# A Nystrom attention and two-layer FFN kernel: the first layer in blocks of 512 tokens across batches, and one store of PSUM banks

## The chip, the cores and the metric

The kernel runs on one core of a Trainium2 chip. The metric is the device time of one execution in microseconds, the median over the runs. Each engine (TensorE = PE, VectorE = DVE, ScalarE = ACT, GpSimd = POOL, and SyncE = SP, which issues all the DMAs here) works through its own list of instructions in a fixed order and waits for the others by semaphores.

## The reference, cut to what matters

Attention with 32 landmarks on 4 batches, 8 heads, 576 positions of 64 values, then two feed-forward layers on 2304 tokens (model width 512, hidden width 2048). All inputs are float64 in the reference.

```python
q_lm = q.reshape(B, H, m, S // m, D).mean(axis=3); k_lm = ...
A, Bm, C = sm(q, k_lm), sm(q_lm, k_lm), sm(q_lm, k)      # softmax of scaled scores
Z = Bm.transpose(0, 1, 3, 2) / (norm_1(Bm) * norm_inf(Bm) + 1e-06)
for _ in range(6):
    Z = 2 * Z - Z @ Bm @ Z
x = (A @ Z @ C @ v)                                      # [B, H, S, D] -> [2304, 512]
h = x @ moe_w_in;  x = (h * np.tanh(softplus(h))) @ moe_w_out
h = x @ moe2_w_in; return (h / (1 + np.exp(-h))) @ moe2_w_out
```

## The kernel before

**Attention** works on eight groups of four heads (`Group`, g = 0 to 7; two groups make a batch). A group loads k and q (`load`) and v (`load_v`), transposes k and q on TensorE (`transposed`, results `Tk` and `Tq`), sums nine pairs of rows into landmarks (`sums` on VectorE or POOL, or for groups 2 and 3 products with the constant `twice` on TensorE), takes scores, exponentials and maxima, and runs six Newton steps on a 32x32 system for each head (`newton`, tile `yu`). `c_side` multiplies the transposed exponentials `ect` with v (mark `cv`). The last product of a group has the operands `bd,yu`; it gives `ut`, the landmark values. `a_side` gives the query weights in a tile `at` for each batch.

**The first layer** never forms the attention output. `projection` multiplies `ut` of a batch with the weights `wa` into landmark weights `wp` (512 hidden columns at a time, a tile of 16 KB in each partition, ring of three). A unit (phase, token block t, hidden tile f) is then `emit_h` (`h<-at,wp`: six matmuls, two head groups times three passes, since every value is split into a high and a low part in the format fp32r, `PASSES`), `gated` (ACT activation `z`, its high part `g` on ACT, its low part on POOL) and `emit_o` (`y<-g,wo`: four output tiles times three passes, twelve matmuls). The hidden width is cut in two halves: phase 0 runs all token blocks over hidden tiles 0 to 7 and stores partial sums `yh`, phase 1 over 8 to 15, reads `yh` back and stores `ys`. A token block of phases 0 and 1 is half a batch, 288 tokens, so eight blocks; phase 2, the second layer, has blocks of 512 (`h<-x,wi`, `y<-wo,g`; four of 512 and one of 256). Weights come as float64 words and are put together by ACT and DVE (`decode`, tiles `m` and `wa`) and split by ACT and POOL.

**What sets the order.** A planner written into the kernel (`Line`) runs while the program is built: it holds a time for each engine and a cost for each instruction and emits what is ready next, so the order on each engine is fixed before the launch. Attention steps are chains that are stepped when their inputs are due; units of the first layer fill in when `h_time` and `o_time` say that they are ready. Where TensorE has nothing and its recent activity is low (`cold`), two transposes of the identity are put in (`y<-ident` and the like). Tiles come from `Ring`s: a taker waits until a slot is given back. PSUM has eight banks: four for `y`, two for `h`, two for attention (`t`); groups 0 and 1 borrow from `y` and `h`. Group 1's q and its transposes are put in the three `wp` slots (`borrow`).

Of the kernel before, what the change touches and what calls it, by code (L numbers as in the profile page):

```python
# [23 lines left out]
SLACK = 0.3  # L24
# [304 lines left out]

@with_exitstack  # L330
def kernel(
# [29 lines left out]
    NB = {0: 2 * B, 1: 2 * B, 2: -(-NT // 512)}  # L361
# [3 lines left out]
    def tokens(ph, t):  # L365
        return (t * SH, SH) if ph < 2 else (t * 512, min(512, NT - t * 512))
# [24 lines left out]
    wp_p = l1.enter_context(tc.tile_pool(name="wp", bufs=3))  # L391
    at_p = l1.enter_context(tc.tile_pool(name="at", bufs=1))
    z_p = l1.enter_context(tc.tile_pool(name="z", bufs=3))
    g_p = l1.enter_context(tc.tile_pool(name="g", bufs=4))
    ps_y = ctx.enter_context(tc.tile_pool(name="ps_y", bufs=4, space=bass.MemoryType.PSUM))
    ps_h = ctx.enter_context(tc.tile_pool(name="ps_h", bufs=2, space=bass.MemoryType.PSUM))
    pctx = ctx.enter_context(ExitStack())
    ps_t = pctx.enter_context(tc.tile_pool(name="ps_t", bufs=2, space=bass.MemoryType.PSUM))
# [142 lines left out]
    lent = []  # L541
    for b in (3, 2):
        words = at_p.tile([128, 4 * GB * SH], I32, tag=f"at{b}", name=f"aw{b}")
        lent += [words[:, i:i + 1024].rearrange("p (n t) -> p n t", t=2) for i in (0, 1024)]
# [14 lines left out]
    def projection(b, fb):  # L559
        keys = [("a", 0, fb * KD + kk) for kk in range(KD)]  # L560
        yield from until(lambda: wp_r.any() and all(w_ready.get(k, LATE) <= line.now for k in keys))
# [13 lines left out]
        wp_ = wp_t[b, fb] = wp_r.take([128, 2, GB, FB], F32R)  # L575
        wp = wp_[0]
        yield "W"
        for e in range(GB):
            VA.copy(out=wp[:, 0, e], in_=pp[e][0])
        yield "V"  # L580
        for e in range(GB):
            V.tensor_tensor(out=wp[:, 1, e], in0=pp[e][0], in1=f32(wp[:, 0, e]), op=ALU.subtract)
            Ring.give(pp[e])
        wp_ready[b, fb] = line.end + 0.12 + SLACK
        yield "W"

    def inputs():

        for t in range(NB[2]):
            n0, n = tokens(2, t)  # L590
            need = [("y", 1, i) for i in range(n0 // SH, -(-(n0 + n) // SH))]
# [17 lines left out]
    def emit_h(ph, t, f):  # L609
        h = h_t[ph, t, f] = h_r.take([128, 512], FP32)  # L610
        n = tokens(ph, t)[1]
        if ph < 2:
            b, e = divmod(t, 2)
            wp, at = wp_t[b, f // 4][0], a_t[b]
            ops = [
                (wp[:, i, k, f % 4 * 128:f % 4 * 128 + 128], at[:, j, k, e]) for k in range(GB) for i, j in PASSES
            ]
        else:
            wi = w_t["i", 1, f]
            ops = [  # L620
                (wi[:, i, k * 128:(k + 1) * 128], x_t[t][k][0][:, j, :n]) for k in range(KD) for i, j in PASSES
            ]
        for i, (w, x) in enumerate(ops):
            T.matmul(out=h[0][:, :n], lhsT=w, rhs=x, start=(i == 0), stop=(i == len(ops) - 1))
            if i % STRIDE == STRIDE - 1:
                yield

    def gated(ph, t, f):

        h = h_t.pop((ph, t, f))  # L630
        n = tokens(ph, t)[1]
        yield from until(z_r.any)
        z_ = z_r.take([128, SH if ph < 2 else 512], FP32)
# [5 lines left out]
        g = g_t[ph, t, f] = g_r.take([128, 2, SH if ph < 2 else 512], F32R)  # L639
# [6 lines left out]
    def emit_o(ph, t, f, first, last):  # L646
        n = tokens(ph, t)[1]
# [3 lines left out]
        if first:  # L651
            y_t[ph, t] = []
        for d in range(parts):
            if first:
                y_t[ph, t].append(y_r.take([128, 512], FP32))
# [16 lines left out]
    def partial(t):  # L672

        yp_t[t] = []
        n0, n = tokens(1, t)
        yield from until(marked(("part", 0, NB[0] - 1)))
# [6 lines left out]
    def finish(ph, t, d):  # L683
        n0, n = tokens(ph, t)
# [54 lines left out]
    class Group:  # L739
        def __init__(self, g):  # L740
            self.g = g
            self.b, self.hg = divmod(g, GB)

            self.banks = h_r if g == 1 else t_r
            self.pairs = y_r if g < 2 else t_r
            self.tT, self.lm = {}, {}

        def load(self):
# [4 lines left out]
            if self.g == 1:  # L753
                self.borrow()
                qn = self.borrowed[0][0][:, 0:J]
# [11 lines left out]
        def borrow(self):  # L767
            self.borrowed = [wp_r.take([128, 32, D], FP32) for i in range(3)]

        def load_v(self):  # L770
            vn = self.vn = qkv_p.tile([96, HG, VI, D], FP32, tag="vn", name="vn")
            src = heads(v, self.b, self.hg).rearrange("h (p i) d -> p h i d", i=VI)
            line.transfer(nc.sync, out=vn, in_=src)
            self.v_at = line.end

        def sums(self, nm, src):

            now, free = line.now, line.free
            lm = self.lm[nm] = s_p.tile([128, 2, D], FP32, tag="lm" + nm, name="lm" + nm)
            if max(now, free["V"]) + 3 < max(now, free["P"]) + 3.4:  # L780
                V.tensor_reduce(out=lm[:, 0, :], in_=src.rearrange("p j d -> p d j"), axis=AX.X, op=ALU.add)
                yield "V"
                V.copy(out=lm[:, 1, :], in_=lm[:, 0, :])
            else:
                t9 = s_p.tile([128, J2, D], FP32, tag="t9", name="t9", bufs=1)
# [471 lines left out]
```

## Time and profile before

| | us |
|---|---|
| median of 3 runs | 874.95 (874.9 to 878.39) |
| the profiled execution | 875.92 |
| its span, first to last instruction | 874.1 |
| TensorE busy | 847.2 (97%) |
| first layer, `y` matmuls, busy | 234.1 (1536 of them) |
| first layer, `h` matmuls, busy | 120.3 (768) |
| second layer, `y` / `h` matmuls, busy | 204.8 / 206.5 |

Attention takes up to about 222 us of the span, with the first layer woven in from 51 us on; the first layer then runs alone until 466 us, and the second layer from there. Matmul records overlap, since one begins before the one ahead of it has drained: a mean length is longer than the distance from start to start, which is what counts in a dense run. `PEld` rows are loads of the stationary operand; every matmul here has one.

### The profile page before, as it was taken

To read this page: it belongs to the slowest core of one execution; us is meant where nothing else is said; L and a number is where in the kernel's file an instruction comes from. 1 tells how busy PE (TensorE), PEld (TensorE's weight loads), DVE (VectorE), ACT (ScalarE), POOL (GpSimd) and SP (SyncE) were. 2 spreads that over 40 slices of the span, in tenths; PEclk is the share of its full clock that TensorE was granted. 3 is DMA by queue.
4 is the path that set the end of the run, shared out by engine and by line. 5 is a ranking of instruction groups with operands and counts; after the bars stand their busy time and mean duration, and the time that the engine had idled before them with its cause. 6 is when DMAs were issued, how large, how long until landed. Compare 5 with 4: busy or idle time off the path is not lost. (4 is left out here: it accounts for less than half of the span.)

```text
span 874.1 us, 15110 instructions
## 1 busy us (share of the span) xinstructions
PE 847.2 (97%) x6036; PEld 718.5 (82%) x6036; DVE 302.0 (35%) x574; ACT 383.8 (44%) x804; POOL 344.4 (39%) x335
## 2 busy tenths in 40 slices
PE   7999999899999999999999999999999999999997
PEld 6777766676999899999998876888888888888896
DVE  4966634543576872010118779300000000000000
ACT  5575767656565553342335445421232123212322
POOL 4241633432455672432337766531233123212221
PEclk8999999999999999999999999999999999999999
DMA  9774225200335532331136900120012000100000
GB/s 250 223 219 152 66 46 136 56 29 5 121 125 189 155 111 64 111 97 56 55 124 227 338 31 1 30 67 1 1 27 58 1 1 24 37 1 1 24 26 25
DMA packets 41863, 72.29 MB, mean 83 GB/s; under 512 B 5184, under 2 KB 29248, under 8 KB 41792
## 3 DMA queue, kind: packets, MB, share of 16 engines
q1 hardware_dynamic: 41792, 71.32, 27.0%
q8 instruction: 47, 0.77, 0.4%
q14 instruction: 24, 0.20, 0.1%
HBM read 57.15 MB, written 14.16 MB: 82 GB/s over the span
## 5 line engine op out<-in xcount | busy, mean ns | idle before, releaser
L221 POOL TENSOR_TENSOR g<-z,g 128x288 fp32r<-128x288 f32 (+2 forms) x208 | 208.1, 1008 | 385.3 <-ACT g L221 325.7
L221 PE MATMUL y<-g,wo 128*128 128x288 f32 x1536 | 234.1, 301 | 0.0
L221 ACT ACTIVATE z<-h 128x288 f32<-128x288 f32 (+2 forms) x208 | 96.0, 468 | 293.1 <-PE h L221 258.0
L221 PEld LDWEIGHTS y<-g,wo 128*128 128x128 f32 x1536 | 209.6, 188 | 12.9 <-issue 9.0
L221 PE MATMUL h<-x,wi 128*128 128x512 f32 (+1 forms) x960 | 206.5, 371 | 0.6 <-POOL wi L221 0.6
L221 PE MATMUL y<-wo,g 128*128 128x512 f32 x864 | 204.8, 392 | 1.2 <-POOL g L221 1.1
L221 PEld LDWEIGHTS h<-x,wi 128*128 128x128 f32 x960 | 167.7, 188 | 34.7 <-POOL wi L221 1.9
L221 PEld LDWEIGHTS y<-wo,g 128*128 128x128 f32 x864 | 161.5, 188 | 38.4 <-POOL g L221 2.5
L221 PE MATMUL h<-at,wp 128*128 128x288 f32 x768 | 120.3, 301 | 5.3 <-ACT z L221 5.2
L221 PEld LDWEIGHTS h<-at,wp 128*128 128x128 f32 x768 | 106.1, 188 | 19.2 <-issue 8.5
L221 ACT CAST g<-z 128x288 fp32r<-128x288 f32 (+2 forms) x204 | 98.2, 490 | 17.5 <-PE y L221 13.9
L221 DVE SCALAR_TENSOR_TENSOR m<-wst,m 128x512 int32<-128x512 int32 x96 | 105.3, 1115 | 1.6
L221 POOL TENSOR_TENSOR wo<-m,wo 128x512 fp32r<-128x512 f32 x32 | 48.2, 1508 | 35.5 <-ACT wo L221 32.0
L221 DVE CAST x<-xst 128x512 fp32r<-128x512 f32 (+1 forms) x4 | 2.9, 721 | 160.8 <-PE h L221 160.8
L221 DVE TENSOR_SCALAR m<-m 128x512 int32<-128x512 int32 x48 | 34.5, 724 | 31.0 <-ACT m L221 31.0
L221 ACT ACTIVATE m<-wst 128x512 f32<-128x512 f32 x48 | 32.4, 675 | 24.8 <-POOL wo L221 11.1
L221 DVE TENSOR_TENSOR ysb<-y,ysb 128x288 f32<-128x288 f32 x32 | 13.3, 457 | 80.5 <-PE y L221 77.1
L221 ACT ACT_TABLE_LOAD x31 | 39.8, 1283 | 1.7 <-PEq L1241 0.7
L221 POOL TENSOR_TENSOR x<-xst,x 128x512 fp32r<-128x512 f32 (+1 forms) x20 | 24.7, 1234 | 35.1 <-ACT x L221 35.1
L221 DVE TENSOR_TENSOR wp<-t,wp 128x512 fp32r<-128x512 f32 x32 | 20.6, 686 | 39.7 <-ACT wp L221 39.6
L221 POOL TENSOR_TENSOR wi<-m,wi 128x512 fp32r<-128x512 f32 x16 | 24.6, 1535 | 14.8 <-ACT wi L221 14.3
L221 ACT CAST wp<-t 128x512 fp32r<-128x512 f32 x31 | 16.7, 590 | 28.8 <-PE t L221 28.8
(159 smaller groups left out, 549.2 us busy)
## 6 DMA issues: line engine op xcount, KB each, us to landing
wst<-in_moe_w_out_dram SPq DMA_DIRECT2D x32, 512.0 KB, 6.5
wst<-in_moe_w_in_dram SPq DMA_DIRECT2D x28, 512.0 KB, 6.2
kn<-in_k_dram SPq DMA_DIRECT2D x32, 144.0 KB, 5.0
vn<-in_v_dram SPq DMA_DIRECT2D x8, 576.0 KB, 6.2
yh<-ysb SPq DMA_DIRECT2D x32, 144.0 KB, 1.9
ysb<-yh SPq DMA_DIRECT2D x32, 144.0 KB, 2.5
ys<-ysb SPq DMA_DIRECT2D x32, 144.0 KB, 2.2
out_dram<-ysb SPq DMA_DIRECT2D x72, 64.0 KB, 1.7
```

The costliest lines, as they stand in the source:

```text
L221: r = getattr(self.nc[e], name)(**kw)
```

## The change

1. Token blocks of phases 0 and 1 are 512 tokens as in phase 2 (`tokens`): four of 512 and one of 256 instead of eight of 288. A block may lie across a batch border; `pieces` cuts it there, and `emit_h` runs its six matmuls for each piece into its own columns of one PSUM bank. The cuts are 512 | 64, 448 | 128, 384 | 192, 320 | 256. A block that touches two batches needs the landmark weights and query weights of both.
2. Landmark weights are kept in halves of 256 hidden columns, in a ring of seven tiles of 8 KB (`WP`) instead of three of 16 KB.
3. All eight PSUM banks are one store (`Banks`); `h`, `y`, attention (`t`) and the idle transposes take from it up to a limit each (`Share`): `h` two (four in phase 2), `y` four, `t` three, or seven where nothing of the first layer is ready, idle one.
4. Group 1's q and its transposes lie in the tiles of the query weights of batches 0 and 1 (`aw`), its v in two tiles of the gating ring `g`. The `z` ring has two tiles for three and the `g` ring three for four, since they are wider.
5. From group 2 on v is loaded by a chain of its own (`later_v`) after the `cv` of the group before, into a single tile. `sums` runs on VectorE alone.

```diff
+class Share:
+    def ready(self, n=1):
+        return len(self.banks.free()) >= n and self.banks.held(self.kind) + n <= self.most()
...
-    def tokens(ph, t):
-        return (t * SH, SH) if ph < 2 else (t * 512, min(512, NT - t * 512))
+    def tokens(t):
+        return t * 512, min(512, NT - t * 512)
+    def pieces(t):
+        n0, n = tokens(t)
+        cuts = sorted({n0, n0 + n} | {b * S for b in range(B) if n0 < b * S < n0 + n})
+        return [(a // S, a % S, a - n0, c - a) for a, c in zip(cuts, cuts[1:])]
...
-    h_r, y_r, ysb_r = Ring("h", ps_h, 2), Ring("y", ps_y, 4), Ring("ysb", y_p, YSB)
-    z_r, g_r, wp_r = Ring("z", z_p, 3), Ring("g", g_p, 4), Ring("wp", wp_p, 3)
-    t_r = Ring("t", ps_t, 2)
+    h_r = Share("h", banks, lambda: 4 if grown else 2)
+    y_r = Share("y", banks, lambda: KD)
+    clock_r = Share("idle", banks, lambda: 1)
+    t_r = Share("t", banks, lambda: 3 if busy() else 7)
+    z_r, g_r, wp_r = Ring("z", z_p, 2), Ring("g", g_p, 3), Ring("wp", wp_p, WP)
...
-            b, e = divmod(t, 2)
-            wp, at = wp_t[b, f // 4][0], a_t[b]
-            ops = [
-                (wp[:, i, k, f % 4 * 128:f % 4 * 128 + 128], at[:, j, k, e]) for k in range(GB) for i, j in PASSES
-            ]
+            ops = []
+            for b, at, to, m in pieces(t):
+                wp, a = wp_t[b, f // 2][0], a_t[b].rearrange("p i k e n -> p i k (e n)")
+                ops += [
+                    (wp[:, i, k, f % 2 * 128:f % 2 * 128 + 128], a[:, j, k, at:at + m], slice(to, to + m), (k, i, j))
+                    for k in range(GB) for i, j in PASSES
+                ]
...
-            if max(now, free["V"]) + 3 < max(now, free["P"]) + 3.4:
-                V.tensor_reduce(out=lm[:, 0, :], in_=src.rearrange("p j d -> p d j"), axis=AX.X, op=ALU.add)
...
+            V.tensor_reduce(out=lm[:, 0, :], in_=src.rearrange("p j d -> p d j"), axis=AX.X, op=ALU.add)
...
-                groups[n].load_v()
+                line.add(groups[n].later_v(), "C")
...
-        return max([wp_ready.get((t // 2, f // 4), LATE)] + [a_ready.get((t // 2, e), LATE) for e in range(GB)])
+        of = [b for b, *_ in pieces(t)]
+        return max([wp_ready.get((b, f // 2), LATE) for b in of] + [a_ready.get((b, e), LATE) for b in of for e in range(GB)])
```

Three places show how the instructions move. In the rows `at_` with a number is the query weight tile of one batch, and `x` at the end counts instructions.

TensorE in phase 1, batches 0 and 1, before, where attention is long done:

```order
L221 MATMUL y<-g,wo 128x288 x36
L221 MATMUL h<-at_1331,wp 128x288 x30
L221 MATMUL y<-g,wo 128x288 x36
L221 MATMUL h<-at_1331,wp 128x288 x6
L221 MATMUL y<-g,wo 128x288 x24
```

The same place after the change (`at_724` is batch 0, `at_1376` batch 1; the block of 512 tokens ends batch 0 after 64):

```order
L221 MATMUL h<-at_724,wp 128x512 x18
L221 MATMUL h<-at_724,wp 128x64 x6
L221 MATMUL h<-at_1376,wp 128x448 x6
L221 MATMUL h<-at_724,wp 128x64 x6
L221 MATMUL h<-at_1376,wp 128x448 x6
L221 MATMUL y<-g,wo 128x512 x2
L221 MATMUL t<-wa,ut_154 32x512 x8
L221 MATMUL y<-g,wo 128x512 x58
```

Every `h` of a block on a border is now two runs of six matmuls, one narrow and one wide, and `y` is wide.

TensorE around the end of group 3 (`bd,yu`), which finishes batch 1, before:

```order
L221 MATMUL t<-yu 32x64 x4
L221 MATMUL h<-at_634,wp 128x288 x2
L221 MATMUL y<-g,wo 128x288 x2
L221 MATMUL t<-Tk,lmT 32x288 x8
L221 MATMUL y<-g,wo 128x288 x20
L221 MATMUL t<-bd,yu 64x128
L221 MATMUL y<-g,wo 128x288 x4
```

And after:

```order
L221 MATMUL h<-at_724,wp 128x512 x2
L221 MATMUL idle<-ident 128x128 x4
L221 MATMUL t<-yu 32x64 x4
L221 MATMUL idle<-ident 128x128 x6
L221 MATMUL t<-ident,lmk 128x128
L221 MATMUL t<-ident,lmq 128x128
L221 MATMUL idle<-ident 128x128 x8
L221 MATMUL y<-g,wo 128x512 x2
L221 MATMUL t<-bd,yu 64x128
L221 MATMUL y<-g,wo 128x512 x6
L221 MATMUL t<-wa,ut_154 32x512 x8
```

Idle transposes now stand where first-layer matmuls of batch 0 stood: the first block is through, and the next one needs batch 1.

VectorE at the start (`lmk`, `lmq` are the landmark sums of k and q, `nmb` the first maximum of a group), before:

```order
L221 TENSOR_REDUCE lmk<-kn 128x64
L221 COPY lmk<-lmk 128x64
L221 TENSOR_REDUCE lmk<-kn 128x64
L221 COPY lmk<-lmk 128x64
L221 TENSOR_REDUCE nmb<-t 128x1
```

And after:

```order
L221 TENSOR_REDUCE lmk<-kn 128x64
L221 TENSOR_REDUCE lmq<-qn 128x64
L221 TENSOR_REDUCE lmk<-kn 128x64
L221 TENSOR_REDUCE lmq<-aw_157 128x64
L221 COPY lmk<-lmk 128x64
L221 COPY lmq<-lmq 128x64
L221 COPY lmk<-lmk 128x64
L221 COPY lmq<-lmq 128x64
L221 TENSOR_SCALAR lmT<-t 128x128 x2
L221 TENSOR_REDUCE nmb<-t 128x1
```

The two sums of q came from POOL to VectorE, and the copies of both groups stand behind all four sums.

## Rows read from the trace of the kernel before

**Rows 1.** The page, parts 1 and 2: all engines, and TensorE's granted clock.
```profile
PE 847.2 (97%) x6036; PEld 718.5 (82%) x6036; DVE 302.0 (35%) x574; ACT 383.8 (44%) x804; POOL 344.4 (39%) x335
PEclk8999999999999999999999999999999999999999
```

**Rows 2.** Groups by shape, first layer on TensorE: busy us, mean ns, idle before.
```profile
L221 PE MATMUL y<-g,wo 128*128 128x288 f32 x1536 | 234.1, 301 | 0.0
...
L221 PE MATMUL h<-at,wp 128*128 128x288 f32 x768 | 120.3, 301 | 5.3 <-ACT z L221 5.2
```

**Rows 3.** Timeline of TensorE, first layer alone: start us, length us, instructions.
```profile
340.19 6.56 PE L221 MATMUL y<-g,wo 128*128 128x288 f32 x48
346.59 0.95 PE L221 MATMUL h<-at,wp 128*128 128x288 f32 x6
```

**Rows 4.** Timeline of TensorE in the second layer, and one piece of the chain.
```profile
599.85 8.54 PE L221 MATMUL y<-wo,g 128*128 128x512 f32 x36
608.22 8.32 PE L221 MATMUL h<-x,wi 128*128 128x512 f32 x36
616.38 8.32 PE L221 MATMUL y<-wo,g 128*128 128x512 f32 x36
...
834.15 5.91 PE L221 MATMUL h<-x,wi 128*128 128x256 f32 x48
839.90 5.76 PE L221 MATMUL y<-wo,g 128*128 128x512 f32 x24
...
561.37 2.72 PE y L221 x12
```

**Rows 5.** Timeline of TensorE, Newton steps of attention between first-layer matmuls.
```profile
215.08 1.06 PE L221 MATMUL y<-g,wo 128*128 128x288 f32 x6
216.07 0.37 PE L221 MATMUL t<-yu 32*32 32x96 f32 x8
216.37 1.06 PE L221 MATMUL y<-g,wo 128*128 128x288 f32 x6
```

**Rows 6.** Weight loads (PEld): three stretches of the timeline, and the group.
```profile
215.08 0.83 PEld L221 LDWEIGHTS y<-g,wo 128*128 128x128 f32 x6
...
210.69 1.10 PEld L221 LDWEIGHTS y<-g,wo 128*128 128x128 f32 x8
...
42.75 2.09 PEld L221 LDWEIGHTS t<-Tk,twice 128*128 128x128 f32 x18
...
L221 PEld LDWEIGHTS y<-g,wo 128*128 128x128 f32 x1536 | 209.6, 188 | 12.9 <-issue 9.0 <-POOL g L221 0.2
```

**Rows 7.** Timeline of TensorE, a run of idle transposes.
```profile
48.65 1.75 PE L221 MATMUL y<-ident 128*128 128x128 f32 x14
```

**Rows 8.** What TensorE waited for: us in total, times, longest.
```profile
PE t L221 <- ACT ec L221: 6.6, 6, 1.5
PE h L221 <- ACT z L221: 5.2, 7, 1.0
```

**Rows 9.** Timeline of VectorE at the start.
```profile
5.53 2.14 DVE L221 TENSOR_REDUCE lmk<-kn 128x64 f32<-128x1152 f32 x1 [3.89 <-DMA kn<-in_k_dram]
...
15.94 0.19 DVE L221 TENSOR_REDUCE nmb<-t 128x1 f32<-128x32 f32 x1 [3.08 <-PE t L221]
```

**Rows 10.** Groups by shape: gating of 512 columns on ACT and POOL.
```profile
L221 ACT CAST g<-z 128x512 fp32r<-128x512 f32 x63 | 39.2, 622 | 1.7
L221 ACT ACTIVATE z<-h 128x512 f32<-128x512 f32 x64 | 38.2, 598 | 182.6 <-PE h L221 153.4 <-POOL g L221 25.1 <-POOL wi L221 4.1
...
L221 POOL TENSOR_TENSOR g<-z,g 128x512 fp32r<-128x512 f32 x64 | 86.0, 1344 | 176.0 <-ACT g L221 135.6 <-issue 29.7 <-PE h L221 9.6
```

**Rows 11.** Timelines of SP's queue and of TensorE: group 2's v.
```profile
24.52 0.33 SPq L232 DMA_DIRECT2D vn<-in_v_dram  x1
...
63.88 0.88 PE L221 MATMUL t<-vn,ect 96*32 96x64 f32 x48
```

More of the change, by code (lines that the diff above doesn't have):

```diff
@@ L327, in give, with __init__, held, free @@
         tile[1][2].append(max(x[2] for k in "wr" for x in Ring.line.seen.get((k, tile[0].name), [(0, 0, 0.0)])))
+class Banks:
+    def __init__(self, pools):
+        self.all = [[p, 1, [], "ps", None] for p in pools]
+    def held(self, user):
+        return sum(not p[1] and p[4] == user for p in self.all)
+    def free(self, late=0.1):
+        now = Ring.line.now + late
+        return [p for p in self.all if p[1] and (not p[2] or p[2][0] <= now)]
+class Share:
+    def __init__(self, kind, banks, most):
+        self.kind, self.banks, self.most = kind, banks, most
+    def ready(self, n=1):
+        return len(self.banks.free()) >= n and self.banks.held(self.kind) + n <= self.most()
+    def any_of(self, n):
+        return sum(p[1] for p in self.banks.all) >= n
+    def take(self, shape, dtype):
+        p = min((p for p in self.banks.all if p[1]), key=lambda p: p[2][0] if p[2] else -1.0)
+        p[1], p[4] = 0, self.kind
+        t = p[0].tile(shape, dtype, tag="ps", name=self.kind)
+        if p[2]:
+            Ring.line.seen["w", t.name] = [(0, 1 << 30, p[2].pop(0), "ring")]
+        return t, p
 @with_exitstack
@@ L560, in projection @@
         keys = [("a", 0, fb * KD + kk) for kk in range(KD)]
-        yield from until(lambda: wp_r.any() and all(w_ready.get(k, LATE) <= line.now for k in keys))
+        yield from until(lambda: wp_r.any_of(2) and all(w_ready.get(k, LATE) <= line.now for k in keys))
         yield from until(lambda: t_r.ready(GB))
@@ L574, in projection @@
         marks.add(("P", b, fb))
[L575 to L584, printed above, removed]
+        for i in range(2):
+            wp_ = wp_t[b, 2 * fb + i] = wp_r.take([128, 2, GB, FB // 2], F32R)
+            wp, c = wp_[0], slice(i * FB // 2, (i + 1) * FB // 2)
+            yield "W"
+            for e in range(GB):
+                VA.copy(out=wp[:, 0, e], in_=pp[e][0][:, c])
+            yield "V"
+            for e in range(GB):
+                V.tensor_tensor(out=wp[:, 1, e], in0=pp[e][0][:, c], in1=f32(wp[:, 0, e]), op=ALU.subtract)
+                if i:
+                    Ring.give(pp[e])
+            wp_ready[b, 2 * fb + i] = line.end + 0.12 + SLACK
         yield "W"
     def inputs():
-        for t in range(NB[2]):
-            n0, n = tokens(2, t)
-            need = [("y", 1, i) for i in range(n0 // SH, -(-(n0 + n) // SH))]
+        for t in range(NT5):
+            n0, n = tokens(t)
+            need = [("y", 1, t)]
             x_t[t] = []
@@ L620, in emit_h @@
             ops = [
[L621 to L624 removed]
+                (wi[:, i, k * 128:(k + 1) * 128], x_t[t][k][0][:, j, :n], slice(0, n), (k, i, j))
+                for k in range(KD) for i, j in PASSES
+            ]
+            last = (KD - 1, *PASSES[-1])
+        for i, (w, x, c, part) in enumerate(ops):
+            T.matmul(out=h[0][:, c], lhsT=w, rhs=x, start=(part == (0, 0, 0)), stop=(part == last))
             if i % STRIDE == STRIDE - 1:
@@ L630, in gated @@
         h = h_t.pop((ph, t, f))
[L631 removed]
+        n = tokens(t)[1]
         yield from until(z_r.any)
[L633 removed]
+        z_ = z_r.take([128, 512], FP32)
         z = z_[0][:, :n]
@@ L651, in emit_o @@
         if first:
-            y_t[ph, t] = []
+            y_t[ph, t] = [y_r.take([128, 512], FP32) for d in range(parts)]
         for d in range(parts):
-            if first:
-                y_t[ph, t].append(y_r.take([128, 512], FP32))
             y = y_t[ph, t][d][0]
@@ L765, in rows @@
                 line.transfer(nc.sync, out=to[32 * i:32 * i + 32].rearrange("p j d -> p (j d)"), in_=of[i])
-        def borrow(self):
-            self.borrowed = [wp_r.take([128, 32, D], FP32) for i in range(3)]
         def load_v(self):
-            vn = self.vn = qkv_p.tile([96, HG, VI, D], FP32, tag="vn", name="vn")
             src = heads(v, self.b, self.hg).rearrange("h (p i) d -> p h i d", i=VI)
-            line.transfer(nc.sync, out=vn, in_=src)
-            self.v_at = line.end
+            if self.g == 1:
+                self.lent = [g_r.take([96, 2, VI, D], FP32) for i in range(2)]
+                tiles = [x[0] for x in self.lent]
+            else:
+                tiles = [qkv_p.tile([96, HG, VI, D], FP32, tag="vn", name="vn", bufs=1)]
@@ L1139, with busy @@
     line.add(inputs(), "S")
+    grown = 0
+    def busy():
+        if flight or banks.held("y") or not todo:
+            return True
+        ph, t, f, *_ = todo[0]
+        return ph < 2 and all(wp_ready.get((b, f // 2), LATE) <= line.now + 3 for b, *_ in pieces(t))
     def h_time(u):
```

106 lines of the change are left out of this document (49 added, 57 removed).

## The prediction

> **What bounds the kernel now.** I read the page first: TensorE is busy for 97% of the span, the other engines for less than half, and the clock is granted in full after the first slice [rows 1]. So the end is set by how many TensorE instructions there are, what each takes, and where TensorE stands still. Then the groups by shape: the first layer is 1536 `y` and 768 `h` matmuls of 288 columns [rows 2]. Their modelled length (301 ns) overlaps, so the pace is read from starts in the timeline: 48 of them from 340.19 to 346.59 us are 6.40 us, 0.133 us each [rows 3]. The second layer gives the pace of other widths: 36 matmuls of 512 columns take 8.37 us or 8.16 us (608.22 - 599.85, 616.38 - 608.22), mean 0.230 us each; 48 of 256 columns take 5.75 us, 0.120 us each [rows 4]. A run of 12 of 512 takes 2.72 us, the same pace as the better long runs [rows 4].
>
> Next, what interleaved attention costs. Six `y` matmuls start at 215.08 and the Newton step behind them at 216.07: 0.99 us where the pace gives 0.80, so a return from attention to the first layer costs 0.19 us more than its matmuls [rows 5]. The weight loads say why. In a run of six loads the whole takes 0.83 us; less the last one's 0.188 us and four intervals of 0.133, the first interval is 0.109 us; the run of eight gives 0.112 [rows 6]. That first interval has no earlier matmul in its way: it is the time of a load of 128x128 of these weights. The 18 loads before `twice` products, 128 columns wide, keep (2.09 - 0.19) / 17 = 0.112 us [rows 6].
>
> **Step 1, `y` in wider blocks.** The order has 768 matmuls of 512 columns and 192 of 256 for the 1536 of 288. Before: 1536 x 0.133 = 204.8 us (0.1333 unrounded). After: 768 x 0.230 + 192 x 0.120 = 199.6. **-5.2 us**, all on TensorE's path. It is small because a matmul of 512 costs nearly its columns: per column 0.45 ns against 0.46.
>
> **Step 2, `h` cut at batch borders.** It stays at 768 matmuls with the same columns in all. For each of 96 sets (16 hidden tiles, six products) there are pieces of 512, 64, 448, 128, 384, 192, 320 and 256 columns. Between 256 and 512 I go straight: 0.120, 0.1475, 0.175, 0.2025, 0.230, sum 0.875 us. The pieces of 64, 128 and 192 are narrower than any fp32r matmul in the trace. From below, the same straight line gives 0.0375 + 0.065 + 0.0925 = 0.195 us; from above, each costs what 256 columns cost, 0.360 together. I take 0.112 each, 0.336 together: every matmul has its own load, six narrow ones come in a row, and a load takes that long [rows 6]. So 96 x (0.875 + 0.336) = 116.3 us against 768 x 0.1333 = 102.4: **+13.9 us**, ends +0.3 and +16.2.
> The Trainium skill (TensorE: Matmul & The Clock Gate, Back-to-back issue gap) gives a sustained 81 ns for 128 columns with its load. By that, as an estimate, the narrow pieces cost 0.243 and this step +4.9, and the kernel would end near 869.6. The same page's section on LDWEIGHTS gives columns over 1.2, 107 ns, which the loads above bear out; its 131 ns for 512 columns is not what this trace shows.
>
> **Step 3, idle transposes and alternation.** The order counts 222 idle transposes for 208. The run of 14 takes 1.75 us, 0.125 each [rows 7]: **+1.8 us**. Runs of the first layer are broken by something else 110 times instead of 128, at 0.19 us [rows 5]: **-3.4 us**.
>
> **Step 4, one bank store.** Attention may hold three banks, or seven where nothing of the first layer is ready, instead of two. The waits this can remove are those of TensorE for a bank that exponentials (6.6 us) or gatings (5.2 us) still read [rows 8]; 11.8 us in all, few of them long. It can also add some, since the new order was laid out for durations that the narrow pieces don't keep. Ends -11.8 and +6; I take **-4 us**, since half of these waits are for the result and not for the bank.
>
> **Step 5, the start.** Key and query sums of groups 0 and 1 now all run on VectorE, and all four reductions stand ahead of the copies. A reduction takes 2.14 us, and the row that follows them, `nmb`, began at 15.94 [rows 9]. Two more are 4.3 us, but VectorE waited for data about that long around them. Group 0 comes later, group 1, the last of the two, hardly: ends -1 and +3, I take **+0.5 us**. Until both groups are through their Newton steps TensorE has nothing else to do, so this counts in full. The later groups' two sums on VectorE lie beside first-layer work.
>
> **Steps at nothing.** Gating is 96 wide units instead of 128: per unit ACT 0.598 + 0.622 = 1.22 us and POOL 1.344 [rows 10], against 1.38 us of TensorE in `h` (6 x 0.230) and 2.76 in `y`; if that cover went, five units in a row would stall for their rings of two and three tiles, about 1 us each time. Landmark weights in halves are twice as many copies and subtractions, hidden as VectorE and ACT are under half busy [rows 1]. The V load of later groups moves behind other loads on the SP queue and waits for the previous group's `cv`; group 2's was issued at 24.52 and read by TensorE at 63.88 [rows 11], so some 30 us are to spare. The second layer keeps its matmuls; runs of 12 in place of 36 keep the pace, and a unit's gating (2.6 us by [rows 10]) has 5.4 us.
>
> **The sum.** -5.2 + 13.9 + 1.8 - 3.4 - 4 + 0.5 = +3.6 us. On the profiled execution's 875.92 us (span 874.1 us, and 1.8 us around it) that is 879.5; the runs' median lies 1.0 us under that execution, so the forecast is **878.5 us**. About 0.5% is what a measurement of this kernel can tell from no change: 870.6 to 879.3.
>
> **Rivals.** *A, the narrow pieces cost only their columns*, because loads are taken ahead further than one matmul. Step 2 is then +0.3, and the time 865. For it: no narrow fp32r matmul stands in the trace. Against it: the loads of [rows 6], which don't come closer. The skill's 81 ns lies between the two.
> *B, slower: the batch border.* A block of 512 no longer ends with its batch, so block 1 waits for batch 1's landmark weights, with only 512 tokens of batch 0 as cover where there were 576. The order itself has 18 idle transposes ahead of group 3's last product and 14 ahead of block 2. From group 3 or 5 being some 2 us later than laid out, TensorE waits there in addition. One border costs up to the four Newton steps left, 1.29 us each (216.37 - 215.08 [rows 5]), about 5 us; two are 10, and the time 888.5. Against it: such steps slip only if VectorE holds them, and it is not full.
> *C, the bank waits all go.* Step 4 is -11.8, and the time 870.7. Against it: a step that waits for an exponential's result is as late with any number of banks.
>
> **How the numbers follow.** Forecast (874 to 883) 0.45, of which 0.10 lies above 879.3; A 0.15; B 0.25; C 0.15, half of it beyond the bound. Faster: 0.15 + 0.08 = 0.23. Same: 0.35 + 0.07 = 0.42. Slower: 0.25 + 0.10 = 0.35. The range reaches to A's and B's times but for their outer halves: 866 to 889. The forecast's own range is 874 to 883, which is what its ends in steps 2 and 5 and half of those in step 4 leave.
>
> **What would show it.** Step 1: `y` of 512 at 0.23 us in the stretch after attention. Step 2: six `h` of 64 columns from start to start in 0.67 us (0.22 would be A), of 128 and 192 likewise. Step 3: the same 0.19 us at returns. Step 4: TensorE's waits for exponentials and gatings under 8 us in sum. Step 5: the last Newton product of group 1 within 3 us of where it was. B: idle time of TensorE before the first `h` of 64 and of 128 columns. The prediction is wrong if narrow pieces run at their columns' pace, if attention ends more than 10 us from where these terms put it, or if the second layer's runs of 12 wait for gating.

## Result and the profile after

| | before | after |
|---|---|---|
| median of 9 runs, us | 874.9 | 880.62 (879.03 to 881.37) |
| the profiled execution / its span, us | 875.92 / 874.1 | 879.03 / 877.2 |
| ratio of the runs | | 1.0052, 95% interval 1.0038 to 1.0065 |

The change makes the kernel slower by half a per cent: 5.7 us on the medians, 4.6 by the ratio. The page of the changed kernel reads like the one before [rows 1]; the first row shows the engines' busy time, the second the granted clock in 40 slices:

```profile
PE 853.1 (97%) x5474; PEld 683.8 (78%) x5474; DVE 304.4 (35%) x603; ACT 368.6 (42%) x724; POOL 313.3 (36%) x258
PEclk8999999999999999999999999999999999999999
```

TensorE is still what the span is made of. So I split its time by kind of work: what each matmul takes from its own start to the next one's start, added up. Waits are in it, put down to the matmul ahead of them. Two more kernels stand in the table, e9 and e10 below: the changed kernel and the one before without the function tables of ACT.

| us up to the second layer | before | after | diff. | before, no tables | after, no tables | diff. |
|---|---|---|---|---|---|---|
| `y` of the first layer | 223.4 | 213.4 | -9.9 | 217.6 | 211.6 | -6.0 |
| `h` of the first layer | 117.4 | 126.2 | +8.7 | 112.4 | 126.0 | +13.6 |
| idle transposes | 30.5 | 35.0 | +4.6 | 29.1 | 34.2 | +5.1 |
| attention, landmark weights | 93.3 | 90.9 | -2.5 | 86.5 | 87.6 | +1.1 |
| all | 464.6 | 465.5 | +1.0 | 445.6 | 459.4 | +13.8 |
| the second layer | 401.9 | 404.2 | +2.3 | 401.9 | 404.6 | +2.8 |

**Paces.** The groups by shape (busy us, mean ns of one, idle time before) answer to [rows 2]:

```profile
L221 PE MATMUL y<-g,wo 128*128 128x512 f32 x768 | 197.9, 402 | 0.3 <-POOL g L221 0.3
L221 PE MATMUL idle<-ident 128*128 128x128 f32 x222 | 35.0, 292 | 2.4 <-POOL ident masks.py:199 1.4 <-ACT eb L221 0.7
L221 PE MATMUL h<-at,wp 128*128 128x192 f32 x96 | 13.8, 274 | 0.0
L221 PE MATMUL y<-g,wo 128*128 128x256 f32 x192 | 24.0, 282 | 0.0
```

As in [rows 3], the pace is read from starts. The timeline of TensorE in the first layer alone (start us, length us; a row joins shapes and names the first) has runs where six narrow pieces and six wide ones follow each other:

```profile
345.03 7.73 PE L221 MATMUL h<-at,wp 128*128 128x64 f32 x48
352.60 0.63 PE L221 MATMUL y<-g,wo 128*128 128x512 f32 x2
...
356.62 2.06 PE L221 MATMUL h<-at,wp 128*128 128x64 f32 x12
358.52 11.40 PE L221 MATMUL y<-g,wo 128*128 128x512 f32 x48
369.76 5.89 PE L221 MATMUL h<-at,wp 128*128 128x64 f32 x40
...
427.33 6.37 PE L221 MATMUL h<-at,wp 128*128 128x192 f32 x48
433.54 11.40 PE L221 MATMUL y<-g,wo 128*128 128x512 f32 x48
```

Twelve matmuls, half of 64 and half of 448 columns, take 358.52 - 356.62 = 1.90 us; at 0.112 and 0.2025 they would take 1.89. The 48 from 345.03 take 7.57 us, 0.158 each, and the mean of the two prices is 0.157. The 48 of 192 and 320 take 6.21 us, 0.129 each, against 0.130. From one start to the next of its like, the median is 112 ns for 64 and 192 columns and 111 ns for 128. Where six of 64 stand together, from the first start to that of the matmul behind them it is 0.58 or 0.69 us. `y` of 512: 48 in 11.24 us (369.76 - 358.52), 0.234 each.

**A stall of TensorE, and what stands behind it.** In the changed kernel (TensorE first, then ACT):

```profile
91.41 1.66 PE L221 MATMUL h<-at,wp 128*128 128x512 f32 x6
...
93.08 0.29 PE L221 MATMUL t<-yu 32*32 32x64 f32 x8
94.73 1.19 PE L221 MATMUL h<-at,wp 128*128 128x512 f32 x4 [1.36 <-ACT z L221]
```

```profile
92.15 0.63 ACT L221 CAST wo<-m 128x512 fp32r<-128x512 f32 x1
92.79 1.28 ACT L221 ACT_TABLE_LOAD   x1
94.09 0.60 ACT L221 ACTIVATE z<-h 128x512 f32<-128x512 f32 x1
```

The gating `z` has its input at 93.07 (91.41 + 1.66), but ACT loads the table for Mish until 94.07, since the last function was an exponential, and the next matmuls of `h` wait for `z`, which still reads the bank. Attention uses exponentials and the first layer Mish, so ACT goes back and forth. All its table loads, in the kernel before and the changed one:

```profile
L221 ACT ACT_TABLE_LOAD x31 | 39.8, 1283 | 1.7 <-PEq L1241 0.7 <-PE h L221 0.4
```

```profile
L221 ACT ACT_TABLE_LOAD x25 | 32.1, 1283 | 4.7 <-PE h L221 3.5 <-PEq L1290 0.7
```

29 of the 31 and 22 of the 25 lie between 45 and 225 us, where attention is mixed with the first layer. The planner has no cost for them (`cost` of ACT knows the function `Ln` alone), so the order was laid out as if they took no time. The prediction counted them nowhere.

TensorE's waits for exponentials and gatings in the changed kernel (us in all, times, longest; `z` is the gating, `eb` an exponential) are 6.1 us, where [rows 8] has 11.8:

```profile
PE h L221 <- ACT z L221: 3.4, 3, 1.4
...
PE h L221 <- ACT eb L221: 1.3, 1, 1.3
...
PE idle L221 <- ACT eb L221: 0.7, 1, 0.7
PE t L221 <- ACT z L221: 0.7, 1, 0.7
```

### The profile page after: what moved, and what is told of

It is laid out like the page before. It is cut to its first block, busy times and chain, and to the rows that moved or that the text cites. A ratio compares the mean times of both kernels' runs of the same rounds, so it can differ in the third digit from the quotient of the medians.

```text
span 877.2 us, 13680 instructions
## 1 busy us (share of the span) xinstructions
PE 853.1 (97%) x5474; PEld 683.8 (78%) x5474; DVE 304.4 (35%) x603; ACT 368.6 (42%) x724; POOL 313.3 (36%) x258
## 4 chain that ended last, share of the span: by engine, by line
PE 85%; ACT 4%; DVE 3%; DMA 2%; issue 2%; POOL 2%; SPq 1%; POOLq 0%; DVEq 0%; ACTq 0%
PE y L221 44%; PE h L221 35%; PE t L221 6%; ACT L221 1%; DMA wst<-in_moe_w_in_dram 1%; PE idle L221 1%; DMA wst<-in_moe_w_out_dram 1%; ACT z L221 1%; SPq L232 1%; DMA kn<-in_k_dram 1%; POOL g L221 1%; POOL wi L221 0%; POOL wo L221 0%; ACT g L221 0%; DVE lmk L221 0%
## 5 line engine op out<-in xcount | busy, mean ns | idle before, releaser
L221 POOL TENSOR_TENSOR g<-z,g 128x512 fp32r<-128x512 f32 (+1 forms) x160 | 195.8, 1225 | 402.8 <-ACT g L221 289.6
L221 PE MATMUL y<-g,wo 128*128 128x512 f32 (+1 forms) x960 | 221.5, 378 | 0.3 <-POOL g L221 0.3
L221 ACT ACTIVATE z<-h 128x512 f32<-128x512 f32 (+1 forms) x160 | 88.9, 556 | 305.5 <-PE h L221 285.9
L221 PEld LDWEIGHTS y<-g,wo 128*128 128x128 f32 x960 | 163.7, 189 | 37.3 <-issue 6.8
L221 PE MATMUL h<-at,wp 128*128 128x512 f32 (+7 forms) x768 | 129.9, 319 | 4.8 <-ACT z L221 3.4
L221 ACT CAST g<-z 128x512 fp32r<-128x512 f32 (+1 forms) x156 | 89.6, 577 | 28.3 <-PE y L221 25.5
L221 DVE TENSOR_TENSOR wp<-t,wp 128x256 fp32r<-128x256 f32 x64 | 23.9, 414 | 63.7 <-ACT wp L221 63.6
L221 PE MATMUL idle<-ident 128*128 128x128 f32 x222 | 35.0, 292 | 2.4 <-POOL ident masks.py:199 1.4
L221 ACT ACT_TABLE_LOAD x25 | 32.1, 1283 | 4.7 <-PE h L221 3.5
L221 PEld LDWEIGHTS idle<-ident 128*128 128x128 f32 x222 | 26.1, 148 | 9.1 <-ACT eb L221 2.7
L221 ACT CAST wp<-t 128x256 fp32r<-128x256 f32 x55 | 18.0, 378 | 20.3 <-PE t L221 18.7
```

What stands on the lines that cost most here:

```text
L221: r = getattr(self.nc[e], name)(**kw)
```

## The experiments

For each kernel two counts stand beside the time. "Waits" is what TensorE takes beyond a matmul's own pace where that is over 0.4 us, summed from 45 us to the second layer. "Loads" are ACT's table loads in the whole program. Before has 17.6 us of waits and 31 loads, after 9.2 us and 25. The expectations of e5, e7 and e8 use a wider count of waits, which gives 24.5 us for e1, 14.4 for e2 and about 17 for the changed kernel.

**e1: blocks of 288 again, the rest of the change kept.**

```diff
-    def tokens(t):
-        return t * 512, min(512, NT - t * 512)
+    WIDE = tuple(min(512, NT - t * 512) for t in range(NT5))
+    BLOCKS = ((SH,) * (2 * B), (SH,) * (2 * B), WIDE)
+    def tokens(ph, t):
+        return sum(BLOCKS[ph][:t]), BLOCKS[ph][t]
...
-    z_r, g_r, wp_r = Ring("z", z_p, 2), Ring("g", g_p, 3), Ring("wp", wp_p, WP)
+    z_r, g_r, wp_r = Ring("z", z_p, 3), Ring("g", g_p, 4), Ring("wp", wp_p, WP)
...
```

> The changed kernel with part 1 undone: first-layer blocks of 288 tokens again (z ring of three, g ring of four, 288 wide), while the bank store, the landmark weights in halves, the lent places and the sums on VectorE stay. Theory N (the narrow h pieces at their load's length, steps 1 and 2 of the prediction): the matmuls of the first layer cost 307.2 us at 0.1333 us each instead of 315.9, so 880.6 - 8.7 = 872, ratio to the kernel before 0.997, and no h or y of the first layer leaves the pace of 0.133 us. Rival W (the changed kernel lost its time to waits at borders and in the second layer, and widths come out even): 879 to 881. If the bank store and the start are worth what steps 3 to 5 say, it also lies 2 to 5 us under the kernel before.

Measured: 875.1 us, 0.9999 of before (0.9983 to 1.0014); waits 17.8 us, 25 loads. Narrow pieces and the slow second layer are gone (400.5 us), 5.5 us less than after where 8.7 were expected. The rest was taken back by waits, which are those of before. So the bank store, the halves of the landmark weights, the lent places and the sums on VectorE together are worth nothing that shows at this width; what each is worth alone was not run. Theory N holds, but not by itself. In e1's profile the granted clock also falls twice (0.57 from 180 to 188 us and from 464 to 468); in those of before and after it does not fall there.

**e2: six blocks, none of whose pieces is narrow.**

```diff
+    BLOCKS = ((320, 512, 320) * (B // 2), (320, 512, 320) * (B // 2), WIDE)
...
```

> The changed kernel with other cuts of phases 0 and 1: blocks of 320, 512, 320, 320, 512, 320 tokens, so that a wide block on a border holds 256 columns of either batch and no h piece is narrower than 256. Theory N: by the paces read (320 columns 0.1475 us, 256 0.120, 512 0.230) the first layer's matmuls cost 96 x (4 x 0.1475 + 4 x 0.120 + 2 x (4 x 0.1475 + 2 x 0.230)) = 304.3 us against 315.9 in the changed kernel, so 880.6 - 11.6 = 869, ratio 0.994. Rival B (blocks across a batch border wait for the later batch, here two of six instead of three of five): idle time of TensorE ahead of the first 512 block grows and eats it, 873 to 880. Rival W: 879 to 881.

Measured: 867.34 us, 0.9902 of before (0.9885 to 0.9919); waits 7.1 us, 19 loads. Its second layer starts at 455.25 us, after's at 466.87: 11.6 us, the figure expected of the paces alone. That the two agree so well is partly chance, since e2 also has 2.1 us of waits and six loads less. But split as in the table above, `h` takes 112.9 us for 126.2, 13.3 less where the paces give 13.6 (102.7 for 116.3). The paces can be read in its timeline:

```profile
338.19 11.40 PE L221 MATMUL y<-g,wo 128*128 128x512 f32 x48
349.42 3.95 PE L221 MATMUL h<-at,wp 128*128 128x256 f32 x28
...
355.60 10.01 PE L221 MATMUL y<-g,wo 128*128 128x512 f32 x60
365.45 2.21 PE L221 MATMUL h<-at,wp 128*128 128x320 f32 x14
```

48 `y` of 512 take 11.23 us; twelve of 512 and 48 of 320 take 9.85 us, and by 0.230 and 0.1475 they would take 9.84. Rival B falls: TensorE has no wait ahead of the first `h` of 256, at 117.40 us, though 12 idle transposes stand among the 60 matmuls before it.

**e3: phase 1 in mirrored order, so that its last block is wide.**

```diff
+    BLOCKS = (WIDE, WIDE[::-1], WIDE)
...
```

> The changed kernel with phase 1 alone cut in mirrored order: the block of 256 tokens first, the four of 512 behind it; phase 0 and the second layer as they are. The pieces are the same in number and width. The weights of the second layer from the fifth hidden tile on take the slots that the last block of phase 1 gives back unit by unit; with a last block of 256 tokens these come back from 449 us on, 17 us before the second layer, with 512 about 33 us before it (before: 288 tokens, 19 us). Theory L (late slots make the stalls of 519 to 545 us, 3.3 us of waits for wi and some 1.5 us at the lower clock): the waits for wi in the second layer go, and the time is 880.6 - 3 to 4.5 = 876 to 877.5. Rival O (the second layer's runs of 12 in place of 36 put gating on POOL ahead of weight splits): waits stay, 880 to 881.

Measured: 880.5 us, 1.0053 of before (1.0034 to 1.0072); 25 loads: no gain. The reason is in several places. In the changed kernel the second layer stalls for weights (TensorE, then POOL, and the windows view with the clock near the end of its row):

```profile
538.74 0.74 PE L221 MATMUL h<-x,wi 128*128 128x512 f32 x2 [0.97 <-ACT wi L221]
540.54 4.05 PE L221 MATMUL h<-x,wi 128*128 128x512 f32 x10 [1.07 <-POOL wi L221]
544.43 1.78 PE L221 MATMUL y<-wo,g 128*128 128x512 f32 x7
```

```profile
538.76 1.73 POOL L221 TENSOR_TENSOR wi<-m,wi 128x512 fp32r<-128x512 f32 x1 [2.21 <-ACT wi L221]
```

```profile
534.70:544.40 9.70, 7.66 (x25) 5.36 (x24) 9.60 (x10) 4.21 (x7) 6.68 (x5) 0.82 0.00 0
```

TensorE stands twice for about 1 us, then ten matmuls take 544.43 - 540.54 = 3.89 us where they need 2.3: six of them come 0.427 us apart, 512 columns at 1.2 GHz, and the clock granted in that stretch is 0.82 of 2.4 GHz on average: 1.00 up to 538.7 us, and 0.50, which is 1.2 GHz, from 540.5 us, where the second one ends. In e3 no wait for `wi` is left and the second layer takes 400.3 us for 404.2. Theory L had that right, though not the time. But a narrow first block of phase 1 runs out of gated tiles, which it shows here:

```profile
307.05 3.70 PE L221 MATMUL y<-g,wo 128*128 128x256 f32 x25
312.72 2.72 PE L221 MATMUL y<-g,wo 128*128 128x256 f32 x11 [1.97 <-POOL g L221]
```

TensorE waits 4.0 us for POOL's `g` in all (1.1 of it in the second layer), 0.3 before the edit. What the end gained the middle lost: in e3's profile the second layer starts 7.2 us later (474.10 for 466.87). 4.8 of these come behind 300.9 us, where the two orders part, from the waits for `g` and a clock of 0.72 from 310 to 316 us. The other 2.4 come from 172 to 180 us, in the same order and behind the same two waits of 0.69 and 1.32 us: there the granted clock is 0.58 and 0.57 in e3's profile, where it is 1.00 in the changed kernel's. The same split of the second layer shows elsewhere: it takes 400.3 to 402.2 us behind a last block of 288, 320 or 512 (before, e1, e2, e3, e10, e12) and 403.4 to 404.6 behind one of 256 (after, e4, e5, e6, e9, e11); only e7 and e8, whose coarser places hold in it too, have 408.

**e4: the planner told what narrow pieces take.**

```diff
+        if e == "T" and kw.get("rhs") is not None and kw["rhs"].dtype == F32R:
+            return max(0.112, self.FIXED[e] + n * self.EACH[e])
```

> The changed kernel with one number of the planner: an fp32r matmul is planned at no less than 0.112 us, so the order is laid out for what 64, 128 and 192 columns take (planned before at 0.040, 0.067 and 0.093). The work is the same. Theory N with drift (the plan runs 13 us ahead of the chip by the end of the first layer, and what was laid out for it comes at the wrong time): 877 to 879.5. Rival (TensorE's list is dense there, and drift costs nothing): 880 to 881.

Measured: 877.2 us, 1.0018 of before (1.0004 to 1.0032); waits 7.5 us, 23 loads. The gain of 3.4 us is the size that drift was to give, but the new order also has two loads fewer. The two are not told apart.

**e5: two banks for attention instead of three.**

```diff
-    t_r = Share("t", banks, lambda: 3 if busy() else 7)
+    t_r = Share("t", banks, lambda: 2 if busy() else 7)
...
-                yield from until(marked((g, "Tk")))
+                yield from until(marked((g, "Tk"), (g, "Tq")))
```

> The changed kernel with attention limited to two banks where the first layer has work, as in the kernel before, instead of three (groups 2 and 3 take their bank for the landmark products only when both transposes are done, since two holders would else block each other). Theory of step 4 (the third bank takes waits of TensorE away): 880.6 + 4 = 884 to 885, and waits of first-layer matmuls for attention return to the 17 us excess that the kernel before has in that stretch. Rival W8 (the 8 us of waits that went came from the wider blocks, since the kernel with the store and blocks of 288 has 24.5 us of them like the kernel before and the one with 320 and 512 has 14.4): 880 to 882, waits about 17 us in sum as in the changed kernel.

Measured: 872.7 us, 0.9962 of before (0.9948 to 0.9976); waits 4.1 us, 19 loads. It is 8 us faster than the changed kernel. Neither theory allowed for that: with a bank less there were fewer waits. That the third bank takes away waits, as step 4 has it, is wrong here. Of the two candidates left, the bank itself or the six loads that the new order has less, e11 decides.

**e6: sums of groups 0 and 1 on POOL where shorter.**

```diff
-            V.tensor_reduce(out=lm[:, 0, :], in_=src.rearrange("p j d -> p d j"), axis=AX.X, op=ALU.add)
+            if self.g > 1 or max(now, free["V"]) + 3 < max(now, free["P"]) + 3.4:
+                V.tensor_reduce(out=lm[:, 0, :], in_=src.rearrange("p j d -> p d j"), axis=AX.X, op=ALU.add)
...
+            else:
...
+                P.tensor_tensor(out=t9, in0=src[:, 0:J2, :], in1=src[:, J2:J, :], op=ALU.add)
...
```

> The changed kernel with the landmark sums of groups 0 and 1 on VectorE or POOL as the planner finds shorter, as in the kernel before (POOL's scratch lies in the free half of batch 0's query weight tile); the later groups keep VectorE. Step 5 of the prediction says that this moves the first Newton chains by -0.5 us (ends +1 and -3): 878 to 881. Group 0's last product was 3.8 us later in the changed kernel (41.39 for 37.59) and group 1's 1.35 us; if the start sets the whole attention stretch, group 1's moves back by 1.3 us and the time with it: 879.3. If the start has slack, group 0 moves and the time does not: 880.6.

Measured: 877.25 us, 1.0004 of before (0.9986 to 1.0021); waits 5.5 us, 21 loads. Group 0's last product comes at 36.48 us for 41.39, group 1's at 44.22 for 43.13, later and not earlier as expected. So on VectorE the start gives group 1 a gain of 1.1 us at the price of 4.9 for group 0, and the time is 3.4 us better without it. But again four loads are gone with it; the start is not shown to be the cause.

**e7 and e8: attention put in only after every third matmul**, in e1 and in e2.

```diff
-STRIDE = 2
+STRIDE = 3
...
-                if i == 2 or (d * 3 + i) % STRIDE == STRIDE - 1:
+                if i == 2:
```

> The kernel of e1 (blocks of 288) with coarser places for attention between first-layer matmuls: after every three matmuls (0.40 us) in place of two or one (0.13 to 0.27), which is about what one or two matmuls of 512 columns take. Theory G (wide blocks lost fewer waits because attention steps are put in at coarser places, so fewer of them come too early): the waits of the stretch fall from 24.5 us to about 17, breaks from 120 to 111, and the time from 875.1 to 868 to 871. Rival (width itself, by more work per gating and per unit, not the places): waits stay at 22 to 26 us, 874 to 876.

> The kernel of e2 (320, 512, 320) with the same coarser places, after every three matmuls (0.44 to 0.69 us). Theory G: breaks fall from 108 to 98, 1.9 us at 0.19 us each, and waits by a few us from 14.4: 862 to 866. Rival (attention's own chain gets longer when its steps have to wait for a place, and idle transposes fill the rest, 244 for 228): 867 to 870.

Measured: e7 887.21 us, 1.0133 of before (1.0115 to 1.015), waits 21.0 us, 27 loads. e8 868.73 us, 0.9917 (0.99 to 0.9934), waits 6.5 us, 19 loads. Theory G falls for blocks of 288: the coarser places cost 12 us, and waits rise from 17.8 to 21.0. But between the profiles only 6.4 us of it lie before the second layer (it starts at 471.95 us for 465.60 in e1); 7.4 lie in it, where the coarser places hold too. e7's list of waits (us in all, times, longest) shows gatings in both parts, the first row before the second layer, and 5.0 of the 6.5 us of the other in it:

```profile
PE h L221 <- ACT z L221: 6.8, 8, 2.2
PE y L221 <- POOL g L221: 6.5, 6, 1.9
```

In e8 the second layer starts 1.6 us earlier than in e2 (453.67 for 455.25) and is 5.4 us longer, so its time is in the rival's range, though before the second layer the coarser places cost it nothing. e7's granted clock also falls to 0.5 in four places (within 134 to 142, 178 to 184, 468 to 474 and 674 to 678 us), and what that costs is in its times.

Across e1 to e8 one thing goes along with the waits better than width, banks or places do: kernels with 19 to 23 loads have 4 to 7.5 us, those with 25 to 31 have 9 to 21.

**e9, e10, e11: no function tables in the first layer**, in after, before and e5.

```diff
-        A.activation(out=z, in_=h[0][:, :n], func=ACTF.Silu if ph == 2 else ACTF.Mish)
+        A.activation(out=z, in_=h[0][:, :n], func=ACTF.Silu if ph == 2 else ACTF.Copy)
```

> The changed kernel with ACT's function for gating in phases 0 and 1 a plain copy in place of Mish (this leaves the Mish out of the output); every instruction of all engines stands in the same order, but the 25 loads of function tables of ACT become 2. Theory T (the waits of TensorE in the attention stretch come behind table loads of 1.28 us that the order was laid out without): the waits of over 0.4 us from 45 us to the second layer, 9.2 us in sum, fall to about 3, and the time by 5 to 8 us, to 873 to 875. Rival (they are steps laid out too early, whatever ACT does): less than 2 us, 879 to 881.

> The kernel before with the same edit (Mish left out of the output; 31 table loads become 2, the order is the same). Theory T: its waits are 17.6 us and fall to about 5, the time by 10 to 13 us, to 862 to 865; then the changed kernel without tables (873 to 875) lies 9 to 11 us behind it, which is step 2 less step 1 (8.7 us) with nothing taken off it, and what made the two kernels come out so near is that the change has fewer table switches. Rival: both fall by the same 0 to 6 us, and the difference between them stays at 5 us.

> The kernel of e5 (attention limited to two banks) with the same edit (Mish left out; 19 table loads become 2). Theory T: the third bank itself is worth nothing, and what e5 gained came with six fewer table switches of the order that it led to: 870 to 873, within 2 us of e9. Rival B (the third bank takes h its second bank, since y holds four of eight): e11 stays 5 to 8 us under e9.

| | time, us | of before | waits, us |
|---|---|---|---|
| e9 (after) | 873.03, 7.6 less | 0.996 (0.9948 to 0.9973) | 9.2 to 3.8 |
| e10 (before) | 857.36, 18.2 less | 0.9785 (0.9763 to 0.9807) | 17.6 to 2.6 |
| e11 (e5) | 871.79, 0.9 less | 0.9952 (0.9933 to 0.9971) | 4.1 to 3.2 |

Theory T's sizes hold for e9 and e11. In e10 they are passed: 857.36 us where 862 to 865 were expected. The waits that went are 5.4 of e9's 7.6 us and 15.0 of e10's 18.2; the rest is not placed. Could Copy simply be a shorter function than Mish? It is not: gating `z` takes as long in before (first row) as in e10 (second row), and all engines have the same instructions in the same order but for the loads:

```profile
L221 ACT ACTIVATE z<-h 128x288 f32<-128x288 f32 (+2 forms) x208 | 96.0, 468 | 293.1 <-PE h L221 258.0 <-POOL g L221 26.1 <-POOL wo L221 4.2
```

```profile
L221 ACT ACTIVATE z<-h 128x288 f32<-128x288 f32 (+2 forms) x208 | 96.1, 468 | 305.3 <-PE h L221 270.4 <-POOL g L221 26.1 <-POOL wo L221 4.2
```

The same stretch of before and of e10 shows what a load does (TensorE of before, ACT of before, TensorE of e10):

```profile
89.96 0.95 PE L221 MATMUL y<-g,wo 128*128 128x288 f32 x6
92.11 0.26 PE L221 MATMUL t<-bt 32*32 32x32 f32 x8 [1.20 <-ACT ec L221]
...
95.29 0.91 PE L221 MATMUL y<-g,wo 128*128 128x288 f32 x5
```

```profile
90.17 1.28 ACT L221 ACT_TABLE_LOAD   x1
91.47 0.50 ACT L221 ACTIVATE ec<-t,nmc 128x288 f32<-128x288 f32 x1
...
92.88 1.28 ACT L221 ACT_TABLE_LOAD   x1
```

```profile
85.90 0.95 PE L221 MATMUL y<-g,wo 128*128 128x288 f32 x6
86.78 0.26 PE L221 MATMUL t<-bt 32*32 32x32 f32 x8
...
89.24 1.04 PE L221 MATMUL y<-g,wo 128*128 128x288 f32 x6
```

From the first `y` of the stretch to the last it is 5.33 us with tables and 3.34 without; the wait for the exponential `ec` is gone. Over the whole program that wait, 6.6 us in [rows 8], is 0.5 in e10, and the one for `z`, 5.2, is 1.6:

```profile
PE h L221 <- ACT z L221: 1.6, 2, 0.8
...
PE t L221 <- ACT ec L221: 0.5, 1, 0.5
```

Without tables the changed kernel is 873.03 - 857.36 = 15.7 us behind, not 5, and not the 9 to 11 expected. And e11 lies 1.2 us under e9, within the intervals: the number of banks matters hardly, and what e5 gained on the changed kernel came with the order, in which the loads cost next to nothing. It is not their number that sets the cost: 17 loads taken out of e5 give 0.9 us, 23 out of after 7.6 and 29 out of before 18.2. That goes with the waits that went, 0.9, 5.4 and 15.0 us.

**e12: a kernel built from what the runs showed**: e2's blocks, e5's two banks, and a planner that charges a table load and holds a change of table back until 2.5 us after the last one.

```diff
+        if table and table != self.table:
+            self.table = table
+            self.switched = at
+            at += 1.28
...
+    def may(self, table):
+        return self.table == table or self.now >= self.switched + 2.5
...
```

> A whole kernel for a better time, from e2 and e5: blocks of 320, 512, 320, two banks for attention, and a planner that knows the table load (1.28 us) and lets ACT change its table only 2.5 us after the last change. The order has 17 table loads. Theory T: the waits of 7.1 us of e2 fall to 3 to 4, and fewer loads lie on the attention chain: 860 to 865. Rival (holding gatings and exponentials back makes the chain longer than the loads did): 867 to 872.

Measured: 858.1 us, 0.9791 of before (0.9768 to 0.9813), the full computation; waits 2.9 us. It is faster than both kernels, by 2.1% (1.9 to 2.3) and 2.6%, and under the 860 to 865 expected. Its page and its loads:

```profile
PE 840.1 (98%) x5684; PEld 699.5 (82%) x5684; DVE 310.6 (36%) x623; ACT 357.4 (42%) x736; POOL 317.2 (37%) x274
```

```profile
L228 ACT ACT_TABLE_LOAD x17 | 21.8, 1283 | 6.5 <-PE h L228 5.5 <-PEq L1307 0.7
```

Of the 17.5 us on before, some 15 are waits (17.6 to 2.9) and 2.9, as an estimate, the first layer's matmuls by their paces (307.2 to 304.3). Idle transposes take 5.5 us more (36.0 for 30.5), which other gains must make up. The three edits stand together here: what charging the loads brings without holding changes back, or without the blocks, was not run.

## Why the prediction came out as it did

The forecast was 878.5 us, the result 880.6, in its own range of 874 to 883 and 1.3 us above 879.3, up to where it called it the same. That range is narrower than the ends it names: step 2's alone go from +0.3 to +16.2. The sum was near; its parts were not all right.

- **Step 1**, -5.2 us: -6.0 in the pair without tables, where waits hide least. Alone, `y` of 512 comes at 0.234, not 0.230 (3 us over 768); being broken less often may pay for it. Right in size.
- **Step 2**, +13.9 us: +13.6 in the same pair. Narrow pieces come 0.111 to 0.112 us apart whatever their width, the time of their load [rows 6], and six of 64 take 0.58 or 0.69 us where 0.67 was the sign. Rival A falls. The estimate of 869.6 rested on the sustained gap in the Trainium skill (TensorE: Matmul & The Clock Gate, Back-to-back issue gap), 81 ns at 128 columns with a load; the trace has 111 here.
- **Step 3**: 222 idle transposes as counted, but +4.6 to +5.1 us where +1.8 was put. Fourteen more at 0.125 explain the 1.8. Most of the rest is time from the start of an idle transpose to the attention step behind it: 9.6 us at 34 such places in e9, 6.7 us at 28 in e10. The size failed: a row of the trace priced the instruction, not the idle stretch that it stands in. A return costs 0.18 us beyond the paces in the median of the changed kernel, near the 0.19. Of the -3.4 us for breaks, the steps from attention's last matmul to the first layer's next one give -2.3 (13.7 us at 97 places for 16.0 at 113, in the attention stretch of e9 and e10).
- **Step 4**, -4 us for the bank store: the step that failed. All waits shrank, from 17.6 to 9.2 us, and of the 11.8 us of [rows 8] for exponentials and gatings 6.1 are left, under the 8 us that the prediction named as its sign. But the waits of [rows 8] were hardly for banks. In e10, with the same order and the same two banks, 9.7 of the 11.8 us are gone with the loads (6.6 to 0.5 and 5.2 to 1.6). The third bank brings nothing that shows (e11 against e9), and with blocks of 288 the store and the parts that came with it leave time and waits as they were (e1 against before). By e9 and e10 tables cost before 18.2 us (875.6 - 857.4) and after 7.6: 10.6 us in favour of the change, the largest gain in the account. The prediction asked whether a wait was for a bank or for a result, and not why the result was late.
- **Step 5**, +0.5 us: group 1's last product moved by +1.35 us (41.78 to 43.13), within the ends. What it is worth is not settled (e6). Attention's last product moved from 221.16 to 224.33 us, within the 10 us named.
- **Steps at nothing**: the second layer costs +2.3 us, up to 2.8. The prediction looked at its runs of 12, which do not wait for gating, as it said. It missed that the last block of phase 1 is now 256 tokens, so weight slots come back late: SyncE issues the weight loads that follow on them from 455.29 us on, 11.6 us ahead of the second layer, where it was 14.6 before and is 24.7 in e3. TensorE stalls for `wi`, and the clock falls behind the stall.
- **Rival B** falls: TensorE's one wait ahead of the first `h` of 64 is 0.75 us, and none of note stands ahead of the first `h` of 128.
- **Rival C** had most of its waits go, 8.4 us, by another cause than its own; losses that no part of the prediction named hid it.

So the total was right in part by chance. The waits gave 10.6 us where 4 were put, and against those 6.6 stood some 9 not seen: 3.3 in idle transposes, 2.8 in the second layer, and 2.6 in attention's matmuls among themselves (57.6 us in e9, 55.0 in e10). The last stands in one pair of profiles only; with tables it is 1.3 less (58.6 for 59.9, waits included), so it is not shown as a cost. The account without tables, +13.8 and +2.8, less the 10.6 of tables, is +6.0; measured are 4.6 by the ratio and 5.7 by the medians. It had to come out near, since the 10.6 are themselves differences of these kernels' times. What in the change led to fewer table loads stays open: e1 has as few with blocks of 288 and still 17.8 us of waits, so where a load falls counts more than how many there are.

## What to carry to other kernels

Price a cut by its narrowest piece: here an fp32r matmul with a load of its own costs at least the load (0.11 us), so cut blocks so that no piece falls under 256 columns (e2: 320 and 256 for 512 and 64). Where an engine's order is laid out in advance, list every instruction that the order will contain, table loads too, and charge them; a wait for "a result of ACT" is worth a look at what ACT did just before. And when a change rearranges an order, compare it with others of the same work before crediting its parts: here single edits moved the time by up to 12 us through the order alone.

## What the hardware showed that was not expected

A table load takes 1283 ns in each of 31 cases in before and 25 in after, and in most of them it is 1.31 us from the end of the instruction of ACT ahead of it to the start of the one behind (92.78 to 94.09 in the stall shown). The Trainium skill (ScalarE: Activation LUTs, What ACT_TABLE_LOAD costs) gives the same 1283 ns and adds a drain of about 1380 ns for each switch. No run here shows a drain of that size beside the load; the measured 1.31 us decides. The Trainium skill's advice there to do all calls of one table set before the next (Table sets: the hidden batching unit) goes with e12, which holds switches back, though e12 doesn't show it by itself.

A stall of TensorE of twice 1 us in the second layer was followed by six matmuls at 1.2 GHz (0.427 us for 0.231), so 2.0 us of waiting cost 1.2 us more. The same happened in e3's profile (172 to 180 us, clock 0.58 and 0.57) and not in the changed kernel's, with the same order and the same waits, and put attention's end 2.4 us later. So a difference of that size between two profiles needs a look at the granted clock before it is given to the edit.
